# Linear attention into a SoLU layer on one core: a fourth chunk on token rows, its sums copied out of PSUM, its products on GpSimd, under a new order table

## The chip, the core and the metric

The kernel runs on one NeuronCore of a Trainium2 chip. Five engines work side by side, each through a queue of its own in strict order: TensorE (PE in the profile, its weight loads PEld), VectorE (DVE), ScalarE (ACT), GpSimd (POOL) and SyncE (SP), which here only issues DMAs. They meet through semaphores. The metric is the device time of one execution in microseconds (us). Three runs of the kernel before took 181.89, 182.10 and 182.81 us, so the median is 182.1 us.

## The reference

Inputs are q, k, v of shape 8 batches x 8 heads x 576 tokens x 64, float32, a norm weight g_norm of 64, and a layer's weights w_in (512 x 1024), w_out (1024 x 512) and g_ln (1024).

```python
kv  = einsum('bhsd,bhse->bhde', k, v)          # 64 x 64 per batch and head
o   = einsum('bhsd,bhde->bhse', q, kv)
x   = o / sqrt(mean(o*o, -1) + 1e-6) * g_norm  # per token and head
x   = x with heads side by side                # 4608 tokens x 512
h   = x @ w_in                                 # 4608 x 1024
u   = h * softmax(h)
out = (u - mean(u)) / sqrt(var(u) + 1e-6) * g_ln @ w_out
```

The whole has 4608 x 512 float32 values of output.

## The kernel before, in words

The tokens are cut into nine chunks of 512. Chunks 0 to 7 are 512 of the 576 tokens of one batch each; chunk 8 collects the 64 tokens that are left of each batch (tile `q_last`, filled by the pieces `ql0` to `ql7`, L175 or L173). Work is cut into named pieces, `o5.0` or `h6.21` for example: letters for the step, then the chunk, then the part. The steps of one chunk are

- `k`, `v`, `q`: loads, issued by POOL (L269), each 576 KB once it is bfloat16; `kv` (L314): k^T v on PE, 144 small matmuls for a whole batch; `kc`: its copies into `kvd` in SBUF;
- q turned so that features lie on partitions. Chunks 0 to 4 do it on PE (`qt`, L359, with copies `qc`). Chunks 5 to 8 do it with a DMA transpose that SP issues (`qx`, L370). All DMA transposes stand behind `gate` (L343), a one-element copy on POOL that waits for the last load, `q7`;
- `o`: q times k^T v into a two-bank PSUM tile, two halves per chunk. Two forms exist, described below; they end in x, the input of the layer;
- `h`: x times w_in on PE (L572 for chunks 0 to 2, L581 for the others), `e`: exp on ACT (L592, L599), `u`: h times exp on DVE (L607, L612), `r`: the squares' sum (L630 on ACT, L632 on DVE, for chunks 3 and up), `st` and `rs`: the row statistics, `t`: u turned by a DMA transpose that SP issues (L637, chunks 3 and up), `a`: times w_out on PE (L767), `b`: the row's scale out of PSUM (L782 ACT, L784 DVE) and `d`: the store (L799 or L801, on SP, POOL or ACT).

From `o` to x there are two forms, and a list, `ROWS_OF_X`, says which chunks have the second.

The first has features on partitions: `o` (L407, 8 matmuls of 256 columns a half), `sq` (L420, ACT), `s` (L435, PE: the heads' means by a matmul), `ln` and `ex` (L439 and L443, ACT), `x` (L453, DVE, from PSUM). It has four parts per chunk.

The second has tokens on partitions: `o` (L470, 32 matmuls of 64 columns a half), `sq` (L479, ACT, 1024 wide), `vd` (L483, DVE: sums per head), `vl` (L489 and L491, ACT), `vg` (L495, POOL: the scale times g_norm, spread to 1024 columns), `x` (L504, DVE: PSUM times that), and `xt` (L512), a DMA transpose of x that SP issues. It has two halves per chunk, and the chunk's stores go as two DMAs of half the size (L799). Chunks 6, 7 and 8 have this form.

What sets the order is one string, `ORDER`: it names every piece once, with its engine after a slash where there is a choice and its buffer after an @. `Plan.run` emits the pieces in that order, so each engine's queue is that string cut down to its pieces. Buffers are named slots: `P0` to `P2` are PSUM tiles of two banks, `S0` and `S1` of one bank, `L`, `M`, `ob` and others are SBUF slots. A piece that takes a slot waits until all users of the slot's last tile are done. The table was found by a search outside the kernel and is pasted in.

Of the kernel before, what the change touches and what calls it, by code (L numbers as in the profile page):

```python
# [8 lines left out]
FP32 = mybir.dt.float32  # L9
# [17 lines left out]
ROWS_OF_X = (6, 7, 8)  # L27
# [53 lines left out]
qc2.0/dve@M0 h1.2+@P1 h1.2 e1.0@M5 u1.0@L5 b0.2/dve@ob2 h1.3+ h1.3 e1.1@M4 u1.1 h1.4+@P0 h1.5+ k4@L3 o2.0@P2
sq2.00@osq0 sq2.01@osq1 r1.0/pool@L0 h1.4 h1.5 qt2.1@S0 e1.2@M3 s2.00@S1 qc2.1/dve ln2.00@lss0 ex2.00@rst1 h1.6+@P1
h1.7+ v4 h1.6 h1.7 e1.3@M7 u1.2 u1.3 s2.01@S1 ln2.01@lss0 a0.30@S0 o2.1@P0 sq2.10@osq1 a0.31 sq2.11@osq0 ex2.01@rst0
s2.10@S1 s2.11@P1 ln2.10@lss1 g1.0@M8 g1.1 g1.2 b0.3/dve@ob0 ln2.11@lss0 a1.00@S0 ex2.10@rst2 ex2.11@rst3 x2.00@M3
q4@M0 k5@L1 v5 x2.01 x2.10 r1.1/pool r1.2/pool r1.3/act ql3/act a1.01 kv3@P2 kc3.1/act qt3.0@S1 x2.11 h2.0@P0 h2.1
h2.2@P1 h2.3 kc3.0/act qc3.0/act@M4 d0.2/sp d0.3/sp kc3.2/act h2.4@P2 h2.5 g1.3 q5@M5 qt3.1@S1 e2.0@M9 g2.0@M7
e2.1@M10 e2.2@M11 u2.0@L4 u2.1 h2.6@P0 h2.7 e2.3@M3 g2.1 g2.2 qc3.1/dve u2.2 k6@L2 qt4.0@S1 o3.0@P1 sq3.00@osq0
qc4.0/dve@M10 r2.0/act@L6 r2.1/pool u2.3 r2.2/act z1@P2 y1 st1 rs1 b1.0/dve@ob0 d1.0/sp a1.10@S1 a1.11 a1.20@P0
r2.3/act s3.00@P2 ln3.00@lss0 a1.21 b1.1/dve@ob2 b1.2/dve@ob1 g2.3 z2@S0 sq3.01@osq0 y2 ex3.00@rst3 st2 o3.1@P2
sq3.10@osq1 s3.01@S1 ln3.01@lss0 a1.30@P0 sq3.11@osq0 ex3.01@rst2 s3.10@S0 ln3.10@lss1 ex3.10@rst0 x3.00@M4 x3.01  # L90
a1.31 a2.00@S1 s3.11@S0 ln3.11@lss0 kv4@P1 ex3.11@rst2 kc4.0/act a2.01 v6 q6@M3 k7@L0 rs2 b1.3/dve@ob3 v7 q7@M7
d1.1/sp d1.2/sp x3.10 kv5@P0 kc4.2/dve kc5.1/act kc4.1/dve o4.0@P1 sq4.00@osq0 x3.11 ql5/pool qt4.1@S0 qc4.1/act
# [32 lines left out]
def kernel(  # L125
# [16 lines left out]
    nc = tc.nc  # L142
# [14 lines left out]
    T = {}  # L157
# [700 lines left out]
```

## Time and profile before

| | |
|---|---|
| median of three runs | 182.1 us (181.89 to 182.81) |
| profiled execution: its time, its span on the core | 181.77 us, 179.7 us |
| PE, DVE, ACT, POOL busy in the span | 164.9, 127.1, 128.1, 71.9 us |
| granted PE clock | 0.999 |
| the last eight matmuls begin at, and take | 173.82 us, 1.04 us |

The profiled execution's own time is 2.07 us more than its span, which runs from the first to the last instruction. A row of the groups reads: source line, engine, operation, what it writes <- what it reads, shape and type, how many; then busy time and the mean of one in ns; then the idle time of the engine just before and what ended it. A matmul of 512 columns shows 379 ns, but matmuls overlap: in a run of them one begins every 0.216 us (16 of them take 3.45 us in the chain). PE's work is counted below at that pace and not from the busy time.

### The profile page before, as it was taken

How to read it: one execution, taken by the hardware profiler on the slowest of the kernel's cores; microseconds unless marked ns; L12 is line 12 of the kernel's file. 1: busy time of each engine (PE TensorE's matmuls, PEld its weight loads, DVE VectorE, ACT ScalarE, POOL GpSimd, SP SyncE). 2: the span in 40 equal slices, each digit the busy share in tenths (PEclk: the TensorE clock that was granted, in tenths of full speed). 3: DMA queues.
4: the chain of work that ended last, by engine and by line, in shares of the span. 5: the costliest groups of instructions: out<-in, count | busy, mean ns of one | idle time of the engine just before them, and what ended most of it. 6: DMA issues, size and time to landing. Idle time of an engine off the chain costs nothing.

```text
span 179.7 us, 4520 instructions
## 1 busy us (share of the span) xinstructions
PE 164.9 (92%) x1808; PEld 81.1 (45%) x1831; DVE 127.1 (71%) x222; ACT 128.1 (71%) x239; POOL 71.9 (40%) x83
## 2 busy tenths in 40 slices
PE   6899958699999999999998999899999999999990
PEld 3344435345435565454443444444445444444450
DVE  2327599258874776667998869999788987948630
ACT  2377794593899687979879898469979746986210
POOL 7941596040899998100140006501132960222000
PEclk9999999999999999999999999999999999999999
DMA  5999999999999999999799999999998689968994
GB/s 170 252 207 275 353 208 209 205 208 222 248 233 232 209 207 198 277 214 206 157 172 203 206 216 220 152 256 245 171 227 239 99 166 248 200 139 215 175 256 125
DMA packets 60424, 37.81 MB, mean 210 GB/s; under 512 B 42140, under 2 KB 55204, under 8 KB 60404
## 3 DMA queue, kind: packets, MB, share of 16 engines
q0 software_dynamic: 15456, 20.16, 58.1%
q1 hardware_dynamic: 44036, 15.87, 44.1%
q10 hardware_dynamic: 912, 1.51, 3.1%
q8 instruction: 14, 0.23, 0.5%
q14 instruction: 6, 0.05, 0.1%
HBM read 32.54 MB, written 9.44 MB: 234 GB/s over the span
## 4 chain that ended last, share of the span: by engine, by line
PE 63%; DMA 22%; DVE 6%; issue 3%; POOL 1%; SPq 1%; ACT 1%; POOLq 0%; DVEq 0%; ACTq 0%
PE ps_S L767 20%; PE ps_P L581 19%; DMA sb_M<-in_q_dram 9%; PE ps_P L572 8%; PE ps_P L767 5%; DMA out_dram<-sb_ob 4%; DMA sb_L<-in_v_dram 4%; DMA sb_M<-sb_M 3%; PE ps_S L359 2%; DVE sb_ob L784 2%; PE ps_P L314 2%; PE ps_P L407 2%; DMA sb_L<-sb_L 2%; PE ps_P L691 1%; PE ps_S L435 1%
## 5 line engine op out<-in xcount | busy, mean ns | idle before, releaser
L767 PE MATMUL ps_S<-w_out_sb,sb_L 128*128 128x512 bf16 x220 | 53.1, 379 | 2.9 <-issue 2.4
L581 PE MATMUL ps_P<-w_in_sb,sb_M 128*128 128x512 bf16 x188 | 42.7, 379 | 1.0 <-ACT kvd L173 0.8
L767 PEld LDWEIGHTS <-sb_L 128*128 128x128 bf16 x280 | 26.4, 98 | 33.4 <-issue 3.3
L612 DVE SCALAR_TENSOR_TENSOR sb_L<-ps_P,sb_M 128x1024 bf16<-128x1024 f32 x24 | 29.1, 1222 | 8.4 <-ACT sb_M L599 8.2
L599 ACT ACTIVATE sb_M<-ps_P 128x1024 f32<-128x1024 f32 x24 | 24.5, 1023 | 8.2 <-PE ps_P L581 7.1
L581 PEld LDWEIGHTS <-sb_M 128*128 128x128 bf16 x192 | 18.7, 98 | 23.3 <-issue 0.9
L495 POOL TENSOR_TENSOR sb_M<-rr,g_rep 128x1024 f32<-128x1024 f32 x6 | 12.3, 2061 | 30.4 <-ACT rr L491 23.7
L572 PE MATMUL ps_P<-sb_M,w_in_sb 128*128 128x512 bf16 x94 | 21.9, 379 | 0.1
L607 DVE TENSOR_TENSOR sb_L<-ps_P,sb_M 128x1024 bf16<-128x1024 f32 x12 | 14.6, 1222 | 8.2 <-ACT sb_M L592 8.2
L453 DVE SCALAR_TENSOR_TENSOR sb_M<-ps_P,g_cols,sb_rst 128x512 bf16<-128x512 f32 x24 | 18.0, 790 | 2.9 <-ACT sb_rst L443 2.6
L784 DVE TENSOR_SCALAR sb_ob<-ps_S,rstd 128x512 f32<-128x512 f32 (+1 forms) x19 | 13.8, 735 | 7.7 <-PE ps_S L767 2.2
L592 ACT ACTIVATE sb_M<-ps_P 128x1024 f32<-128x1024 f32 x12 | 12.2, 1024 | 6.9 <-PE ps_P L572 6.9
L643 POOL TENSOR_TENSOR sb_M<-sb_M 128x512 bf16<-128x512 f32 x12 | 15.1, 1278 | 4.9 <-ACT sb_M L592 4.8
L420 ACT ACTIVATE sb_osq<-ps_P 128x512 bf16<-128x512 f32 x24 | 13.4, 596 | 4.6 <-PE ps_P L407 4.6
L630 ACT ACTIVATE sb_M<-sb_L 128x1024 bf16<-128x1024 bf16 x14 | 14.6, 1047 | 0.0
L572 PEld LDWEIGHTS <-w_in_sb 128*128 128x128 bf16 x96 | 9.2, 98 | 10.5 <-issue 0.2
L801 POOL DMA_DIRECT2D out_dram<-sb_ob x10 | 6.3, 633 | 16.4 <-DVE sb_ob L784 8.8
L632 DVE SCALAR_TENSOR_TENSOR sb_M<-sb_L 128x1024 bf16<-128x1024 bf16 x10 | 12.8, 1276 | 0.1
L443 ACT ACTIVATE sb_rst<-sb_lss 128x512 f32<-128x512 f32 x20 | 12.0, 632 | 0.1
L767 PE MATMUL ps_P<-w_out_sb,sb_L 128*128 128x512 bf16 x47 | 11.4, 379 | 0.1
L206 PE MATMUL ps_S<-zeros 128*128 128x512 bf16 (+1 forms) x18 | 8.5, 591 | 1.8 <-DVE zeros L188 1.5
L624 POOL TENSOR_TENSOR sb_L<-sb_L 128x1024 bf16<-128x1024 bf16 x4 | 7.6, 1910 | 6.1 <-DVE sb_L L607 6.0
(96 smaller groups left out, 211.2 us busy)
## 6 DMA issues: line engine op xcount, KB each, us to landing
out_dram<-sb_ob SPq DMA_DIRECT2D x14, 256.0 KB, 4.2
sb_L<-in_k_dram POOLq DMA_DIRECT2D x6, 576.0 KB, 12.2
sb_L<-in_v_dram POOLq DMA_DIRECT2D x6, 576.0 KB, 13.1
sb_M<-in_q_dram POOLq DMA_DIRECT2D x6, 576.0 KB, 12.3
out_dram<-sb_ob POOLq DMA_DIRECT2D x10, 256.0 KB, 4.8
sb_L<-in_moe_w_out_dram POOLq DMA_DIRECT2D x2, 1024.0 KB, 15.8
out_dram<-sb_ob SPq DMA_DIRECT2D x10, 128.0 KB, 3.0
sb_M<-in_q_dram POOLq DMA_DIRECT2D x4, 288.0 KB, 7.0
```

Source lines behind the costliest of these rows:

```text
L420: nc.scalar.activation(out=t[:, :], in_=T["o", c, hf][:, z], func=AF.Square)
L453: nc.vector.scalar_tensor_tensor(out=T["x", c][:, pairs_of(c, hf), :, z], in0=T["o", c, hf][:, z].rearrange("p (n q) -> p n q", n=2), scal ...
L572: nc.tensor.matmul(t[:, f % 2], w_in_sb[:, dt, f * 128:(f + 1) * 128], T["x", c][:, dt].rearrange("p q z -> p (q z)"), start=(dt == 0), st ...
L581: nc.tensor.matmul(T["h", c, m][:, half], x_block(c, m, dt), w_in_sb[:, dt, half * 512:half * 512 + 512], start=(dt == 0), stop=(dt == NP ...
L599: nc.scalar.activation(out=t.rearrange("p a b -> p (a b)"), in_=T["h", c, m].rearrange("p a b -> p (a b)"), func=AF.Exp, accum_out=T["zsum ...
L607: nc.vector.tensor_tensor(out=flat(T["u", c][:, 2 * p:2 * p + 2, :]), in0=flat(T["h", c, p]), in1=flat(T["e", c, p]), op=MUL)
L612: nc.vector.scalar_tensor_tensor(out=T["un", c][:, m, :], in0=T["h", c, m].rearrange("p a b -> p (a b)"), scalar=1.0, in1=T["e", c, m].rea ...
L630: nc.scalar.activation(out=unused, in_=src, func=AF.Square, accum_out=by)
L632: nc.vector.scalar_tensor_tensor(out=unused, in0=src, scalar=1.0, in1=src, op0=MUL, op1=MUL, accum_out=by)
L643: nc.gpsimd.tensor_tensor(out=T["es", c][:, n, :], in0=e[:, 0, :], in1=e[:, 1, :], op=ADD)
L767: nc.tensor.matmul(T["acc", c, m][:, 0], T["u", c][:, f, m * 128:(m + 1) * 128], w_out_sb[:, f, :], start=(f == 0), stop=(f == NF - 1))
L784: nc.vector.tensor_scalar_mul(out=t[:, :], in0=src, scalar1=T["rstd", c][:, m:m + 1])
```

## The change

Chunk 5 joins chunks 6, 7 and 8 in the second form, with tokens on partitions. In that form a new piece `oc` copies each half's 128 x 1024 sums from PSUM to an SBUF tile in float32, on ACT or DVE as the table says (DVE for oc5.0, oc6.0, oc7.0, oc8.0 and oc8.1; ACT for oc5.1, oc6.1 and oc7.1). The product that makes x leaves DVE: GpSimd makes it from the copy, right behind `vg` in its queue. The PSUM tile is then free once `sq` and `oc` have read it. And the order table is another one from end to end: the searched table's engines, slots and order differ in nearly every place.

```diff
-ROWS_OF_X = (6, 7, 8)
+ROWS_OF_X = (5, 6, 7, 8)
...
+    def o_out(c, hf, engine):
+        T["os", c, hf] = room(("os", c, hf), [128, 1024], FP32)
+        copy(engine, T["os", c, hf][:, :], T["o", c, hf].rearrange("p x i -> p (x i)"))
+
     def x_rows(c, hf):
         if hf == 0:
             T["xr", c] = room(("xr", c), [128, 2, 1024], BF16)
-        nc.vector.tensor_tensor(
-            out=T["xr", c][:, hf], in0=T["o", c, hf].rearrange("p x i -> p (x i)"),
-            in1=T["rg", c, hf].rearrange("p i e -> p (i e)"), op=MUL,
+        nc.gpsimd.tensor_tensor(
+            out=T["xr", c][:, hf], in0=T["os", c, hf][:, :], in1=T["rg", c, hf].rearrange("p i e -> p (i e)"), op=MUL
         )
...
+            plan.add("oc" + n, ("act", "dve"), lambda e, hf=hf: o_out(c, hf, e), ["o" + n], [("M", ("os", c, hf))], [("o", c, hf)])
...
-            plan.add("x" + n, "dve", lambda hf=hf: x_rows(c, hf), ["vg" + n] + [f"x{c}.0"] * hf, [] if hf else [("M", ("xr", c))],
-                     [("o", c, hf), ("rg", c, hf)] + [("xr", c)] * hf)
+            plan.add("x" + n, "pool", lambda hf=hf: x_rows(c, hf), ["vg" + n, "oc" + n] + [f"x{c}.0"] * hf,
+                     [] if hf else [("M", ("xr", c))], [("os", c, hf), ("rg", c, hf)] + [("xr", c)] * hf)
```

Four stretches of the new table that are spoken of below. Around the second half of chunk 1:

```diff
-... o1.0@P2 warm8@S0 wc3 sq1.00@osq0 sq1.01@osq1 kv1b@P1 ... a0.00@S0 ... qt1.1@S1 kc1b.0/dve s1.00@P0 s1.01@P1 ...
+... o1.0@P2 warm8@S1 sq1.00@osq0 ... s1.00@S1 sq1.01@osq1 s1.01@P1 ... qt1.1@S0 ... kv1b@P0 ... a0.00@S1 ...
```

Around the first DMA transposes and chunk 5's `o`, cut down to SP's queue, POOL's queue and PE's queue:

```diff
-SP:   ... d0.1 d0.2 d0.3 d1.0 d1.1 d1.2 t3.0 t3.1 qx5 qx6 t3.2 ...
+SP:   ... d0.0 d0.1 d1.0 t3.0 qx5 t3.1 t3.2 d1.2 qx6 qx7 t3.3 t4.0 t4.1 t4.2 xt5.0 d2.3 xt5.1 qx8 t4.3 xt6.0 ...
-POOL: ... q7 ql5 d1.3 gate gb d2.2 ql7 vg6.0 vg6.1 d3.1 d3.2 d4.0 vg7.0 d4.1 vg7.1 vg8.0 vg8.1 d5.1 ...
+POOL: ... q7 gb d0.2 d0.3 ql1 gate d1.1 d1.3 d2.0 d2.1 vg5.0 x5.0 d2.2 vg5.1 d3.0 x5.1 ql5 vg6.0 x6.0 d3.2 vg6.1 x6.1 vg7.0 x7.0 d4.0 vg7.1 d4.2 x7.1 d4.3 vg8.0 x8.0 d5.0 vg8.1 d5.1 x8.1 d5.2 ...
-PE:   ... h4.30 h4.31 o5.0 a2.31 a3.00 ... kv6 o5.1 a3.10 ... o6.0 o6.1 ... a4.01 h5.00 h5.01 kv7 ...
+PE:   ... h3.31 s4.10 a2.20 a2.21 a2.30 s4.11 a2.31 a3.00 a3.01 o5.0 o5.1 kv7 a3.10 h4.00 ... a3.31 o6.0 o6.1 o7.0 a4.00 a4.01 a4.10 h5.00 ...
```

DVE's queue in the stretch in which GpSimd now makes x:

```diff
-DVE:  ... vd6.0 b3.2 x5.10 x5.11 vd6.1 x6.0 ql6 r4.3 kc7.0 st4 x6.1 u5.0 r5.0 ... x7.0 b5.0 vd7.1 vd8.0 b5.2 r6.1 vd8.1 x7.1 x8.0 st6 x8.1 u7.0 ...
+DVE:  ... oc6.0 vd6.0 ql2 st4 oc7.0 vd6.1 u5.0 u5.1 vd7.0 oc8.0 oc8.1 vd7.1 vd8.0 vd8.1 b4.2 u5.2 u5.3 r5.2 u6.0 ... u6.3 st5 b5.0 b5.1 u7.0 u7.1 r6.0 r6.2 st6 r7.0 u7.2 ...
```

And the end, where the last chunk's two half-width stores change queues:

```diff
-... b8.3|0/dve@ob1 d8.2/act b8.3|1/dve@ob2 d8.3|0/act d8.3|1/sp
+... b8.3|0/dve@ob4 a8.3|1@S1 b8.3|1/dve@ob3 d8.2/act d8.3|0/sp d8.3|1/sp
```

PE has 88 instructions more than before, POOL 17 more, DVE 4 fewer, ACT 1 fewer, and SP as many.

104 lines of the change are left out of this document (52 added, 52 removed).

## The prediction

> **What bounds the kernel now.** I read the page's busy lines and slices first, then the chain that ended last, then the groups by form, and then the queues of DVE, POOL and SP where the change touches them.
>
> ```profile
> PE 164.9 (92%) x1808; PEld 81.1 (45%) x1831; DVE 127.1 (71%) x222; ACT 128.1 (71%) x239; POOL 71.9 (40%) x83
> ...
> PE   6899958699999999999998999899999999999990
> ...
> DVE  2327599258874776667998869999788987948630
> ACT  2377794593899687979879898469979746986210
> POOL 7941596040899998100140006501132960222000
> ...
> DMA packets 60424, 37.81 MB, mean 210 GB/s; under 512 B 42140, under 2 KB 55204, under 8 KB 60404
> ```
>
> PE is at nine tenths in nearly all slices; DVE and ACT fill many slices of the second half to eight or nine; POOL is nearly idle from about the twentieth slice on. The chain tells PE's own pace and the places where it stood:
>
> ```profile
> 31.68 0.32 PE ps_S L767
> 32.00 1.73 issue
> 33.73 0.59 PE ps_S L767 x2
> ...
> 45.97 0.34 PE ps_P L407 x8
> ...
> 49.67 0.21 PE ps_S L435
> ...
> 54.80 0.70 PE ps_P L314 x72
> ...
> 61.23 0.45 PE ps_S L359 x8
> ...
> 64.19 1.23 PE ps_P L691 x80
> ...
> 92.04 5.72 DMA sb_M<-sb_M
> ...
> 97.81 0.41 PE ps_P L407 x8
> ...
> 115.31 0.37 ACT kvd L173
> ...
> 115.72 8.79 PE ps_P L581 x40
> ...
> 125.31 0.45 PE ps_P L470 x32
> ...
> 131.04 3.45 PE ps_S L767 x16
> ```
>
> A 512-column matmul starts every 3.45/16 = 0.216 us. Counting PE's whole queue at the paces of such rows gives 152.9 us of work: 137.6 from the first `a0.00` (it begins at 31.6) to the last matmul's end (174.9), so waits in that stretch are 143.3 - 137.6 = 5.7 us. Of these 1.73 are the stop at 32.0, where nothing in the kernel is waited for; about 0.4 stand before 97.81 (`o5.0`, for the DMA transpose `qx5`) and 0.75 before 115.72 (`h5.10`, behind late copies of `kv7`). A kernel that waits so little can win 5.7 us at the very most there and can lose without limit. What counts is which waits the new table removes and which it makes.
>
> **Chunk 5's form.**
>
> ```profile
> L420 ACT ACTIVATE sb_osq<-ps_P 128x512 bf16<-128x512 f32 x24 | 13.4, 596 | 4.6 <-PE ps_P L407 4.6
> L439 ACT ACTIVATE sb_lss<-ps_S 128x512 f32<-128x512 f32 x13 | 7.7, 598 | 0.8 <-PE ps_S L435 0.7
> L443 ACT ACTIVATE sb_rst<-sb_lss 128x512 f32<-128x512 f32 x20 | 12.0, 632 | 0.1
> L453 DVE SCALAR_TENSOR_TENSOR sb_M<-ps_P,g_cols,sb_rst 128x512 bf16<-128x512 f32 x24 | 18.0, 790 | 2.9 <-ACT sb_rst L443 2.6 <-ACT sb_rst L447 0.2
> L479 ACT ACTIVATE sb_rst<-ps_P 128x1024 bf16<-128x1024 f32 x6 | 6.0, 1016 | 1.1 <-PE ps_P L470 1.1
> L483 DVE TENSOR_REDUCE ms<-sb_rst 128x16 f32<-128x1024 bf16 x6 | 7.2, 1212 | 1.2 <-ACT sb_rst L479 1.2
> L504 DVE TENSOR_TENSOR sb_M<-ps_P,sb_M 128x1024 bf16<-128x1024 f32 x6 | 7.2, 1215 | 0.0
> L592 ACT ACTIVATE sb_M<-ps_P 128x1024 f32<-128x1024 f32 x12 | 12.2, 1024 | 6.9 <-PE ps_P L572 6.9
> L607 DVE TENSOR_TENSOR sb_L<-ps_P,sb_M 128x1024 bf16<-128x1024 f32 x12 | 14.6, 1222 | 8.2 <-ACT sb_M L592 8.2
> L489 ACT ACTIVATE lv<-ms 128x16 f32<-128x16 f32 x6 | 1.3, 213 | 0.2 <-DVE ms L483 0.2
> L643 POOL TENSOR_TENSOR sb_M<-sb_M 128x512 bf16<-128x512 f32 x12 | 15.1, 1278 | 4.9 <-ACT sb_M L592 4.8
> L624 POOL TENSOR_TENSOR sb_L<-sb_L 128x1024 bf16<-128x1024 bf16 x4 | 7.6, 1910 | 6.1 <-DVE sb_L L607 6.0
> ```
>
> On PE, 2 x 0.34 for `o` and 4 x 0.215 for the head means go, and 2 x 0.45 come: 0.68 + 0.86 - 0.90, or 0.64 us less. PE is the bound, so this counts in full: **-0.6**.
>
> ACT loses 4 x (596 + 598 + 632) = 7.3 us and gets 2 x (1016 + 2 x 213) = 2.9 and three copies. No copy of 128 x 1024 float32 out of PSUM is in the trace; ACT's exp of that shape takes 1.02 us, so 3.1: ACT ends 1.3 lighter. DVE loses 4 x 790 + 6 x 1215 = 10.4 us and gets 2 x 1212 and five copies at most at the 1222 of a product of that size: 8.5, so 1.9 lighter. Both reliefs lie beside PE and I price them at nothing by themselves; PE's work covers them, and without that cover they would be worth at most their 1.3 and 1.9.
>
> POOL gets two more `vg` and eight products. Each product reads two SBUF tiles of 1024: 1.9 us by the bfloat16 row, at most 2 x 1278 by the float32 row of half that width. I take 1.9, as width and operand count are the same there: about 19 us more on POOL, nearly all after 97. POOL has that much idle time, but the two are now one after the other, so x is ready 1.9 - 1.2 = 0.7 us later after `vg`, and a store on POOL's queue that waits for its `b` holds the next product up. In the new queue `x7.0` has `d4.0`, `x8.0` has `d5.0` ahead of what follows; all have their `b` in time as I walk the queue.
>
> The transpose `xt5` adds two entries to SP's queue and chunk 5's stores become eight halves instead of four. They stand beside PE with several us to spare, except `xt5.0`, which waits behind `t4.2`; I count it at nothing (its end of the range is +1 us, if `h5.00` has to wait for it).
>
> **The head.** In the new table `s1.00`, `s1.01` and `qt1.1` come before `kv1b`. That is 2 x 0.215 + 0.45 = 0.88 us of work. The stop of 1.73 us at 32.0 stands after some 700 instructions of PE; PE's queue holds the same up to `o1.0`, so the 700th now lies inside `kv1b`. If the stop ends at the same time, 33.7, PE has by then done 0.88 more, and lacks the rest of `kv1b` and one matmul: **-0.4**. The ends are nothing and -1.7 (the stop is gone).
>
> **Chunk 5's `o` and the first transposes.** `o5.0` waited for `qx5`, which stands behind `gate`, which waits for the last load.
>
> ```profile
> 88.83 0.18 POOL L343 COPY sb_L<-sb_M 1x1 bf16<-1x1 bf16 x1 [13.32 <-DMA sb_M<-in_q_dram]
> ```
> ```profile
> 89.04 2.84 SPq L637 DMA_TRANSPOSE sb_L<-sb_L  x2
> 92.04 4.10 SPq L370 DMA_TRANSPOSE sb_M<-sb_M  x1
> ```
>
> `qx5` was issued at 92.04 and landed at 97.77, 5.7 us later. The new order issues it behind one transpose instead of two (1.4 us sooner), and four stores (256 KB each) that were issued before the last load now come after it; at the page's mean of 210 GB/s a store is 1.2 us, so the gate opens 0 to 5 us sooner. I take half, 2.5: `qx5` lands at 97.77 - 1.4 - 2.5 = 93.9, and 0.4 later as it now shares the DMA engines with those stores. But the new table also puts `o5.0` earlier: PE has 73.6 us of work ahead of it instead of 77.2, and with the 0.4 from the head it is ready near 97.4 - 3.6 - 0.4 = 93.4. So the wait is about 0.9 instead of 0.4: **+0.5**, from -0.4 (the gate opens early) to +2.6 (it doesn't).
>
> **PSUM tiles.** With the copy a half's tile is free after `sq` and `oc` instead of after `x`; 2 to 3 us of holding go. But `sq` now decides, and ACT's queue is full there: `o7.1` takes the slot of `o7.0`, whose square is the last of six ACT instructions of 1024 columns (with `sq6.0`, `oc6.1`, `sq6.1`, `e5.0`, `e5.1`), with `vl6.0`, `rs4` and `b4.0` between: 6 x 1.02 + 0.8 + 0.6 = 7.5 us, and ACT comes to them about 1.2 us late, behind three squares' sums of chunk 4. PE has ten pieces of 4 x 0.216 = 0.86 us there, 8.6. With a few tenths for ACT's own waits: **+0.3** (0 to 0.9). In chunk 3, `s3.10` now waits for `ln3.01`. ACT has between the end of `h2.7` and that point 1 exp, 2 copies (0.37 each), 2 squares of 1024 (as L479), 4 `sq`, 2 `ln` and 1 `ex`: 1.0 + 0.7 + 2.0 + 2.3 + 1.2 + 0.6 = 7.8 us; PE has `kv3`, `a1.10` to `a1.21`, both `o3`, two head means, `z2` and `a1.30`: 0.7 + 3.5 + 0.7 + 0.4 + 1.2 + 0.9 = 7.4 us. **+0.4**. Against these, the 0.75 before 115.72 came from DVE's queue ahead of `kv7`'s copies, which is rearranged: **-0.75**.
>
> **POOL and DVE at once.** This is the step on which I put most weight, because the trace shows that the two engines block each other.
>
> ```profile
> L632 DVE SCALAR_TENSOR_TENSOR sb_M<-sb_L x10: 1212/1222/1781, 86.5 to 165.9; 128x1024 bf16<-128x1024 bf16 x10
> ```
> ```profile
> L495 POOL TENSOR_TENSOR sb_M<-rr,g_rep x6: 1892/1901/2878, 107.9 to 142.8; 128x1024 f32<-128x1024 f32 x6
> ```
> ```profile
> 111.91 1.51 DVE L175 COPY q_last<-sb_M 128x256 bf16<-128x256 bf16 x1
> ```
>
> The squares' sum on DVE takes 1.22 us, and 1.78 in the one case that began while POOL made a `vg`; the `vg` behind it took 2.88 instead of 1.90; and a copy from SBUF to SBUF that takes 0.22 elsewhere took 1.51 beside another `vg`, just ahead of the copies of `kv7`. Products out of PSUM (L504, L607) don't show this. The Trainium skill (SBUF — State Buffer, Who interferes with whom) gives the rule: a DVE instruction with two SBUF inputs, or in a two-port mode, and a GpSimd instruction that reads SBUF lock each other out for a whole instruction. The trace agrees, by 0.56, 0.98 and 1.29 us.
>
> From `vg5.0` to `x8.1` POOL now has 16 such instructions, 30 us of a stretch of some 45. In DVE's queue `ql2`, `st4`, `r5.2`, `st5`, `r6.0`, `r6.2` and `st6` fall into it: seven meetings, with a chance of 30/45 and half an instruction, 0.95 us, each: 4.4 us of delay on DVE, and each `r` that comes first holds POOL up by as much as 1.2. DVE is at eight to nine tenths there, so a part of it reaches PE through `u` and the P slots: `u6.0` behind `r5.2` is the place that I find, for `h6.30` takes the slot that `u6.0` frees. I take **+1.0**, a quarter, as the seven meetings have slack of 1 to 3 us but for that one; the ends are 0 and 4.4.
>
> **The tail.**
>
> ```profile
> 174.02 0.48 DVE L784 TENSOR_SCALAR sb_ob<-ps_S,rstd 128x256 f32<-128x256 f32 x1 [1.85 <-PE ps_S L774]
> ```
> ```profile
> 174.32 2.46 ACTq L799 DMA_DIRECT2D out_dram<-sb_ob  x4
> ```
>
> Both last half-width stores go on SP: four issues of 2.46/4 = 0.61 one after the other from 174.50, so the last begins at 176.3 where ACT's last began near 176.1: **+0.2** (0 to 0.5).
>
> **The sum** against the profiled execution, 181.77: -0.64 - 0.4 + 0.5 + 0.3 + 0.4 - 0.75 + 1.0 + 0.2 = +0.6, or 182.4. That run stands 0.33 under the median of 182.1, so on the median's scale I forecast **182.7 us**.
>
> **Rivals.** First, *the table carries it* (faster): none of the added waits comes, since the gate opens 5 us sooner and the meetings of DVE and POOL fall into slack. Then -0.64 - 0.4 - 0.4 - 0.75 + 0.2 is -2.0, and 180.1 us; with part of the waits some 180.8. For it speaks that DVE and ACT are lighter and that PSUM is freed sooner; against it that only 5.7 us of waits exist. Second, *the lock decides* (slower): DVE's delay of 4.4 us reaches PE whole, 182.7 + 3.4 = 186.1; with half of it, 2.2, 183.9. It decides once DVE's slack between two `u` is below one POOL instruction, 1.9 us. POOL's low share in the slices speaks against it, DVE's digits for it. The Trainium skill (GPSIMD Engine Reference, Performance versus the Vector engine) speaks against the move as well: it has about 2.5 cycles an element for two inputs, which for 1024 elements at its 1.2 GHz is an estimate of 2.1 us a product and 1.8 us more on POOL in all; no run so far shows this product. Third, *the gate doesn't move*: the wait for `qx5` is 2.1 us longer than I take it, 184.8. Against it: four stores really do move behind the last load.
>
> **How the numbers follow.** Chances: the forecast's case (181.7 to 183.8) 0.40, the table carries it 0.32, the lock decides 0.15, the gate doesn't move 0.13. A measurement here tells 0.5% from no change, that is 181.2 to 183.0. Of the first case 0.24 lie within that and 0.16 above; of the second 0.30 are below it and 0.02 within; the others are above. So faster 0.30, same 0.26, slower 0.44. The range from 180.2 to 185.6 leaves out the far ends of the rivals, about 2 in 10.
>
> **What the profile after would show.** The sum is right if PE's waits after its first `a` are 6 to 7 us; if L470 shows 256 matmuls and L435 20; if DVE's L632 and its SBUF copies show several instructions far above 1.22 and 0.22 us beside POOL's; if `gate` runs at 86 to 87; and if the stop near 33 is under 1 us. It is wrong if the product on POOL takes clearly more than 1.9 us without DVE beside it, if the last load lands at 88.7 as before, or if a long stop at "issue" stands in another place of PE's queue.

## The result, and the profile after

The changed kernel takes **190.87 us** (median of 4 runs, 189.18 to 192.88) against 182.45 for the kernel before on the same chip (181.89 to 183.34): a ratio of 1.0426, with a 95% interval of 1.0337 to 1.0514. Forecast were 182.7 us, with a range up to 185.6. The loss is some 8 us.

The profiled execution is the slowest of the four (192.88 us, span 191.1), and the four differ in TensorE's granted clock: its mean was 0.999 in the run of 189.18 and 0.968 in this one. So a part of the 11.4 us between the two profiled spans, and of the waits below, belongs to that one execution.

The page of the changed kernel, with the same rows as before and the one of the granted clock:

```profile
PE 169.0 (88%) x1852; PEld 82.6 (43%) x1875; DVE 128.5 (67%) x217; ACT 128.5 (67%) x238; POOL 98.5 (52%) x103
...
PE   6789978999999998999499995999759999989990
...
PEclk9999999999999999999969998899988999999998
DMA  5999999999999999997999999946498499999994
...
L508 POOL TENSOR_TENSOR sb_M<-sb_M,sb_M 128x1024 bf16<-128x1024 f32 x8 | 18.9, 2357 | 2.8 <-ACT sb_M L634 2.5
...
L636 DVE SCALAR_TENSOR_TENSOR sb_M<-sb_L 128x1024 bf16<-128x1024 bf16 x10 | 17.0, 1728 | 0.1
```

VectorE and ScalarE are hardly changed. GpSimd is 26.6 us busier, of which the eight products are 18.9. What is new on TensorE are the holes in its row, at slices 20, 25, 29 and 30, and a clock below 9 behind each. Where in the span that is, and how much, is read from stretches of 12 us. The columns are the stretch, its length, each engine's busy time (and instructions), the granted clock, the DMA share and the rate. Before:

```profile
core 0: us, PE busy (x) PEld busy (x) DVE busy (x) ACT busy (x) POOL busy (x), PEclk, DMA share, GB/s
86.00:98.00 12.00, 11.58 (x60) 5.14 (x59) 11.44 (x22) 10.07 (x19) 2.81 (x4) 1.00 0.89 173
98.00:110.00 12.00, 11.68 (x195) 5.78 (x191) 9.52 (x17) 11.19 (x24) 1.90 (x1) 1.00 1.06 216
110.00:122.00 12.00, 11.20 (x121) 5.20 (x120) 11.36 (x19) 7.29 (x18) 3.13 (x3) 1.00 1.13 198
...
sum 72.00, PE 69.99 PEld 33.07 DVE 62.61 ACT 57.05 POOL 20.55; mean PE 11.66 PEld 5.51 DVE 10.44 ACT 9.51 POOL 3.43
```

The same of the changed kernel (both run on to 158):

```profile
86.00:98.00 12.00, 9.03 (x170) 4.57 (x170) 8.26 (x16) 6.71 (x13) 2.84 (x5) 0.96 0.91 211
98.00:110.00 12.00, 11.95 (x49) 5.19 (x50) 9.85 (x19) 10.93 (x24) 7.97 (x6) 0.90 1.19 200
110.00:122.00 12.00, 9.93 (x128) 4.39 (x129) 7.83 (x15) 7.25 (x14) 6.90 (x5) 0.86 1.10 199
...
134.00:146.00 12.00, 8.81 (x33) 3.52 (x32) 9.77 (x13) 5.64 (x14) 7.58 (x6) 0.86 0.89 204
...
sum 72.00, PE 63.19 PEld 28.75 DVE 55.35 ACT 49.93 POOL 42.74; mean PE 10.53 PEld 4.79 DVE 9.23 ACT 8.32 POOL 7.12
```

In the 72 us from 86 on TensorE idles 8.8 us where it idled 2.0, and the clock's deficits (0.04 + 0.10 + 0.14 + 0.14) x 12 make another 5.0. Together that is 11.8 us more, about the whole difference of the spans. In the 86 us ahead of them TensorE is busy 78.28 us against 78.11, so the loss does not lie there. What TensorE waited for from 85 to 158, in the view of its waits:

```profile
PE ps_P L585 <- DVE sb_L L616: 3.3, 3, 2.2
PE ps_P L470 <- DMA sb_M<-sb_M: 2.8, 1, 2.8
PE ps_P L585 <- DMA sb_M<-sb_M: 2.0, 1, 2.0
```

These are three long stops: `o5.0` for the transposed load of q5 (2.8), `h5.00` for the transposed x of chunk 5 (2.0), and `h6.30` for `u6.0` on VectorE (2.2 of the 3.3). Behind each TensorE runs at half clock: after the third, 8 matmuls of 512 columns take 3.56 us, 0.44 each instead of 0.216. A clock of 0.86 over 12 us is 3.4 us at half (0.14 x 12 / 0.5), and costs 1.7. The chain through the first two, followed back from 120 us:

```profile
78.89 7.50 DMA out_dram<-sb_ob
...
88.06 7.66 DMA sb_M<-sb_M
...
95.76 0.71 PE ps_P L470 x64
...
110.75 5.88 DMA sb_M<-sb_M
...
116.67 3.65 PE ps_P L585 x10
```

Of 38 us of this chain 21 are three transfers: a store of 7.5 us, which holds an output buffer that ScalarE needs, q5's transpose (7.7) and the first of chunk 5's x (5.9). The DMA row of the page is at 9 in all of these slices but one (the nineteenth). It was so before the change too (at 9 in every slice from 90 to 134 us):

```profile
DMA  5999999999999999999799999999998689968994
```

The third stop is the one at which VectorE and GpSimd block each other; VectorE's timeline, then GpSimd's:

```profile
136.61 3.63 DVE L636 SCALAR_TENSOR_TENSOR sb_M<-sb_L 128x1024 bf16<-128x1024 bf16 x1
...
140.18 1.21 DVE L616 SCALAR_TENSOR_TENSOR sb_L<-ps_P,sb_M 128x1024 bf16<-128x1024 f32 x1
```

```profile
136.79 2.36 POOL L508 TENSOR_TENSOR sb_M<-sb_M,sb_M 128x1024 bf16<-128x1024 f32 x1
```

`r5.2`, 1.22 us alone, takes 3.63: the product's 2.36 lies whole inside it, and `u6.0` waits behind.

### The profile page after: what moved, and what is told of

Its sections match the earlier page's. It is cut to its first block, busy times and chain, and to the rows that moved or that the text cites. A ratio compares the mean times of both kernels' runs of the same rounds, so it can differ in the third digit from the quotient of the medians.

```text
span 191.1 us, 4622 instructions
## 1 busy us (share of the span) xinstructions
PE 169.0 (88%) x1852; PEld 82.6 (43%) x1875; DVE 128.5 (67%) x217; ACT 128.5 (67%) x238; POOL 98.5 (52%) x103
## 4 chain that ended last, share of the span: by engine, by line
PE 40%; DMA 26%; issue 10%; DVE 10%; ACT 7%; POOL 3%; SPq 1%; DVEq 0%; POOLq 0%
PE ps_S L771 13%; PE ps_P L585 12%; DMA sb_M<-sb_M 9%; DMA sb_M<-in_q_dram 8%; PE ps_P L576 6%; DMA sb_L<-in_v_dram 4%; DMA out_dram<-sb_ob 4%; DVE sb_L L616 3%; DVE sb_M L636 2%; PE ps_P L771 2%; DVE ms L483 2%; ACT sb_M L603 2%; SPq L641 1%; POOL sb_M L647 1%; DVE a L718 1%
## 5 line engine op out<-in xcount | busy, mean ns | idle before, releaser
L771 PE MATMUL ps_S<-w_out_sb,sb_L 128*128 128x512 bf16 x229 | 56.5, 383 | 1.0 <-issue 0.4
L585 PE MATMUL ps_P<-w_in_sb,sb_M 128*128 128x512 bf16 x188 | 47.8, 405 | 6.4 <-DVE sb_L L616 3.3
L771 PEld LDWEIGHTS <-sb_L 128*128 128x128 bf16 x280 | 26.6, 98 | 31.8 <-issue 1.9
L495 POOL TENSOR_TENSOR sb_M<-rr,g_rep 128x1024 f32<-128x1024 f32 x8 | 15.2, 1903 | 24.4 <-ACT rr L491 16.8
L508 POOL TENSOR_TENSOR sb_M<-sb_M,sb_M 128x1024 bf16<-128x1024 f32 x8 | 18.9, 2357 | 2.8 <-ACT sb_M L634 2.5
L453 DVE SCALAR_TENSOR_TENSOR sb_M<-ps_P,g_cols,sb_rst 128x512 bf16<-128x512 f32 x20 | 15.2, 789 | 3.0 <-ACT sb_rst L443 2.6
L636 DVE SCALAR_TENSOR_TENSOR sb_M<-sb_L 128x1024 bf16<-128x1024 bf16 x10 | 17.0, 1728 | 0.1
L420 ACT ACTIVATE sb_osq<-ps_P 128x512 bf16<-128x512 f32 x20 | 11.0, 596 | 2.8 <-PE ps_P L407 2.8
L175 DVE COPY sb_M<-ps_P 128x1024 f32<-128x1024 f32 (+1 forms) x7 | 7.4, 1067 | 7.1 <-PE ps_P L470 3.4
L479 ACT ACTIVATE sb_rst<-ps_P 128x1024 bf16<-128x1024 f32 x8 | 8.0, 1028 | 5.0 <-DVE sb_M L175 5.0
L786 ACT ACTIVATE sb_ob<-ps_S,rstd 128x512 f32<-128x512 f32 x15 | 9.9, 682 | 1.6 <-PE ps_S L771 1.3
```

Of the source, the lines that this page charges most:

```text
L453: nc.vector.scalar_tensor_tensor(out=T["x", c][:, pairs_of(c, hf), :, z], in0=T["o", c, hf][:, z].rearrange("p (n q) -> p n q", n=2), scal ...
L495: nc.gpsimd.tensor_tensor(out=t[:, :, :], in0=T["rr", c, hf][:, :, None].to_broadcast([128, 16, D]), in1=g_rep[:, None, :].to_broadcast([1 ...
L508: nc.gpsimd.tensor_tensor(out=T["xr", c][:, hf], in0=T["os", c, hf][:, :], in1=T["rg", c, hf].rearrange("p i e -> p (i e)"), op=MUL)
L585: nc.tensor.matmul(T["h", c, m][:, half], x_block(c, m, dt), w_in_sb[:, dt, half * 512:half * 512 + 512], start=(dt == 0), stop=(dt == NP ...
L636: nc.vector.scalar_tensor_tensor(out=unused, in0=src, scalar=1.0, in1=src, op0=MUL, op1=MUL, accum_out=by)
L771: nc.tensor.matmul(T["acc", c, m][:, 0], T["u", c][:, f, m * 128:(m + 1) * 128], w_out_sb[:, f, :], start=(f == 0), stop=(f == NF - 1))
```

## The experiments

Each ran beside the kernel before, whose median in the five groups was 182.2 to 182.6.

### One suspect at a time

The first theory was that the product on GpSimd makes the loss, by way of VectorE's blocked instructions. The rivals were the slow clock, the stores ahead of q5's load, and the new table itself.

**one_input**

```
-  nc.vector.scalar_tensor_tensor(out=unused, in0=src, scalar=1.0, in1=src, ..., accum_out=by)
+  nc.vector.tensor_reduce(out=by, in_=src, op=ADD, axis=mybir.AxisListType.X)
```

> The changed kernel, but every squares' sum on DVE (ten of them) is a plain sum of the same tile with one SBUF input instead of the product of two; so the sum of squares and with it the variance is left out for those rows, and the row statistics' first term has its sign turned. The plain sum of that width took 1.21 us on DVE in all eight cases of the changed kernel, beside GpSimd or not. Theory A (GpSimd's products lock DVE out): the 3.6 us instruction becomes 1.2, the pause of PE of 2.6 us before h6.30 goes and with it the half clock behind it, in all 3 to 5 us: 186 to 188. Theory B (the late DMA transposes of chunk 5 cost the time, the lock only uses up slack): the pauses before o5.0 and h5.00 stay and the time is 189.5 to 191.5. Under both, the pauses before o5.0 (2.8) and h5.00 (2.0) stay.

Measured: 190.47 us, ratio 1.045 (1.040 to 1.050). All ten of these sums took 1.21 to 1.22 us, so the blocking of `r5.2` was gone, and the time was not. TensorE's waits from 85 to 158:

```profile
PE ps_P L585 <- DMA sb_M<-sb_M: 3.8, 2, 2.7
PE ps_P L470 <- DMA sb_M<-sb_M: 2.4, 1, 2.4
PE ps_S L771 <- DVE vare L724: 1.8, 1, 1.8
```

The stop moved on by one piece of TensorE's queue: h of chunk 7 now waits 2.7 us for its transposed x, and the clock goes to half behind that one. The blocking decides the place of a stop, and hardly the end.

**filled**

```
+  plan.add(f"fill{i}", "pe", lambda i=i: fill(i), ...)   # 12, 10 and 10 matmuls of zeros
-  o5.0@P2 ... h5.00@P2 ... h6.30@P0
+  fill0@P2 o5.0@P2 ... fill1@P2 h5.00@P2 ... fill2@S0 h6.30@P0
```

> The changed kernel, with 12, 10 and 10 matmuls of zeros (0.216 us each, 6.9 in all) put into PE's queue where it paused: before o5.0, before h5.00 and before h6.30. Nothing is left out. Theory C (a pause of PE of over 2 us is followed by 3.4 us at half clock, which costs 1.7 us each): the clock stays at 1.0 through, the waits themselves stay, and the time is near that run of the changed kernel that had a mean clock of 0.999, 189.2: 188.5 to 189.7 instead of a median of 190.9. The rival (the half clock comes from elsewhere, such as the load on the chip): the three stretches at 0.5 stay and the time is 190.5 to 192.

Measured: 190.32 us, ratio 1.044 (1.039 to 1.049), mean clock 0.999: the half-clock stretches were gone, and the ratio is no lower than the 1.043 of the changed kernel. So the slow clock follows the pauses, and with it gone the loss stays. How much it costs by itself this run cannot tell, since the fills take time too: `o5.0` began at 96.55 behind its fill and at 95.76 without it, `h5.00` at 117.59 and at 116.67.

**stores_later**

```
-  d1.1/pool ... d1.3/pool d2.0/pool ... d2.1/pool ... x5.1 xt5.1 ql5/pool
+  ... x5.1 xt5.1 d1.1/pool d1.3/pool d2.0/pool d2.1/pool ql5/pool     (4 output buffers more)
```

> The changed kernel, but the four stores d1.1, d1.3, d2.0 and d2.1, which GpSimd issues just behind the gate, stand behind x5.1 in its queue (with four more store buffers, so that nothing waits for them). Theory B1 (these stores share the DMA engines with qx5 and hold it up: it took 7.7 us to land instead of 5.7): qx5 lands 1.5 to 2 us sooner, PE's pause before o5.0 falls from 2.8 to about 1 us, no half clock follows, and the time falls by 3 to 3.7: 187 to 188. Rival (qx5 is slow because of SP's own queue and the transposes ahead of it): it lands at 95.7 as before and the time stays at 189.5 to 191.5.

Measured: 189.17 us, ratio 1.035 (1.028 to 1.043). The pause before `o5.0` fell from 2.8 to 0.1 us, but the one before `h5.00` grew from 2.0 to 3.1, with the half clock behind it. That was the first sign of what the loss is: with the four stores elsewhere in the same full stretch, another transfer was late.

**old_table_gpsimd**

```
   # the kernel before and its table; chunks 6 to 8:
+  plan.add("oc" + n, ("act", "dve"), lambda e, hf=hf: o_out(c, hf, e), ["o" + n], [("M", ("os", c, hf))], ...)
-  plan.add("x" + n, "dve", ...)
+  plan.add("x" + n, "pool", ...)
```

> The kernel before with its own table and three chunks on token rows, and one part of the change alone: the sums of chunks 6, 7 and 8 are copied out of PSUM behind sq (oc6.0, oc7.0, oc8.0 and oc8.1 on DVE, oc6.1 and oc7.1 on ACT) and GpSimd makes the product from the copy behind vg. Theory A (the product on GpSimd costs the time wherever it stands): slower than before by 2 to 5 us, 184.5 to 187.5, with L632's instructions on DVE over 2 us beside it. Rival (the new table and chunk 5's transposes cost the time): 182 to 183.5, as DVE is lighter by six products of 1.2 and heavier by four copies of 1.2.

Measured: 190.43 us, ratio 1.049 (1.042 to 1.056). Put like this into a table that was not made for it, the new form of three chunks costs as much as the whole change. The next group takes it apart.

### The form's parts, in both tables

**old_table_copies**

```
   # old_table_gpsimd, but
-  nc.gpsimd.tensor_tensor(out=T["xr", c][:, hf], in0=T["os", c, hf][:, :], ...)
+  nc.vector.tensor_tensor(out=T["xr", c][:, hf], in0=T["os", c, hf][:, :], ...)
```

> The kernel before, its table kept, with the six copies of the sums of chunks 6 to 8 to SBUF added (three on ScalarE, three on VectorE, about 1.1 us each) and the product still on VectorE, which reads the copy in place of PSUM. If GpSimd's product made the 8 us of the kernel that had the same copies and the product on GpSimd, this one is 182 to 184.5: the copies are 3.3 us of work on each of two engines that are busy two thirds of the time. If copying is what delays the chain of chunks 6 to 8, it is above 187.

Measured: 189.08 us, ratio 1.037 (1.029 to 1.045). The six copies of 1.0 to 1.2 us, together with products that read them from SBUF, already cost 6.6 us in the old table; the run does not part the two. Its timeline of TensorE shows one stop of 3.25 us at 140.7, behind an eviction on VectorE (line 788), which stands behind copies and sums of squares in that queue. One product on VectorE, which now reads SBUF alone, took 2.92 us beside GpSimd's scale; the six out of PSUM had 1.215 on the mean.

**old_table_one_input**

```
   # old_table_gpsimd with the sum of one_input
```

> The old table with copies and products on GpSimd (190.4 us), the sum of squares on VectorE replaced by a sum with one input (the sum of squares is left out, the sign of its use turned). If VectorE's waits beside the product (L636 2.94 and 2.81, L718 1.97, L724 1.82 us, against 1.2 and 0.1 to 0.2 alone) are the cost, it comes to 184.5 to 187. If the cost is the longer chain on GpSimd itself (scale 1.9 us, product 2.36 us, then a transpose of 5.2 us, ahead of h of the same chunk), it stays at 188.5 to 191.

Measured: 188.44 us, ratio 1.035 (1.031 to 1.039), 2.0 us under the kernel that it is made from: by the medians VectorE's blocked sums are a quarter of the loss in that table.

**product_on_vector**

```
   # the changed kernel, but
-  plan.add("x" + n, "pool", ...)      nc.gpsimd.tensor_tensor(...)
+  plan.add("x" + n, "dve", ...)       nc.vector.tensor_tensor(...)
```

> The changed kernel with one thing undone: the products of chunks 5 to 8 are made on VectorE again (line 508), from the same copy in SBUF, at the same places of the same table. If the product's place on GpSimd is the cause, whether by the time it takes there (2.36 us), by GpSimd's queue behind it or by VectorE waiting beside it, most of the 8 us comes back: 182.5 to 185.0. If the cause is the rest of the change (the new table, chunk 5's transposed load, the copies), it stays at 187 to 191; VectorE then has 8 products more, about 1.2 us each, on a queue that is busy 128 of 189 us.

Measured: 201.26 us, ratio 1.105 (1.099 to 1.112), a miss for both theories. In this table the product on GpSimd is 10 us better than on VectorE, where it stands at its place in the queue and holds up the sums and evictions behind it (2.1 us of VectorE's idle time are products waiting for the scale, and the trace has GpSimd's next scales wait 33.5 us and ScalarE's exps 13.3 us for these products; that this makes the 10 us is my reading, and no run shows it). So "the product went to the slower engine" is no account of the loss.

**latency**

```
   # the changed kernel with one_input's sum and stores_later's order, and
-  t4.1 t4.2 vg5.0@M2 x5.0@M12 xt5.0@M0
+  vg5.0@M2 x5.0@M12 xt5.0@M13 t4.1 t4.2
```

> The changed kernel with three of its waits taken away together: the sum of squares with one input (no long VectorE wait before h6.30), the stores of chunks 1 and 2 off the SP and GpSimd queues ahead of the load of q5 (d1.1, d1.3, d2.0, d2.1 behind x5.1), and xt5.0 ahead of t4.1 and t4.2 on SP. If the waits add up, each counted once, 2.8 before o5.0, 2.0 before h5.00 and 3.2 before h6.30 with the slow clock behind them (1.7 each): 182 to 185. If a wait that is taken away is replaced by the next product's (h7.00 waiting for xt7.0, as the run with one input had it), 186.5 to 189.

Measured: 188.19 us, ratio 1.032 (1.024 to 1.040). Three waits were taken away and, by the medians, 2.7 us came back. At 110.7 TensorE now stopped 2.2 us for the transposes of u in chunk 4 that `xt5.0` had passed, and at 138.1 it stopped 2.5 us for VectorE's u.

### Leaving the chain out

**no_copies**

```
-  ... oc5.0/dve@M1 ... oc8.1/dve@M8
-  in0=T["os", c, hf][:, :], in1=T["rg", c, hf]...
+  in0=T["rg", c, hf]..., in1=T["rg", c, hf]...
```

> The changed kernel without the eight copies out of PSUM (five on VectorE at 1.22 us, three on ScalarE at 1.0): GpSimd multiplies the scale with itself, so that its instructions keep their number, shape and place. The sums' content is left out. If the work of the copies on the two filled engines is what makes the time (six of them in the old table gave +6.6 us without any product on GpSimd), it comes to 183 to 186. If the length of the chain on GpSimd (1.9 + 2.36 us) and the transposes behind it make it, it stays at 188.5 to 191.

Measured: 188.78 us, ratio 1.035 (1.029 to 1.041). By the medians the copies are worth some 2 us in the new table, but the intervals of the two ratios overlap.

**no_product**

```
-  vg5.0@M2 x5.0@M12 ...  vg8.1@M10 ... x8.1
-  nc.sync.dma_start_transpose(T["x", c][:, hf], T["xr", c][:, hf])
+  nc.sync.dma_start_transpose(T["x", c][:, hf], T["os", c, hf][:, :])
```

> The changed kernel with the scale and the product left out for chunks 5 to 8: the copy out of PSUM writes the bf16 rows itself, and the transpose reads them. The norm of q k^T v and its gains are left out; copies, sums of squares, transposes, stores and the table stay. If GpSimd's part of the chain (4.3 us for each half of a chunk, its queue, and VectorE's waits beside it) is what makes the time, nearly all of it goes: 181 to 184.5. If the copies, the order of the stores and loads, or the transposes themselves make it, it stays at 186 to 190.

Measured: 194.82 us, ratio 1.067. Slower with work left out was an artefact: a copy's slot was now held until the transpose had read it, and an instruction of chunk 6 on ScalarE waited 7.4 us for that slot. It is mended in **no_product_slots**:

```
-  oc7.0/dve@M6 ...
+  oc7.0/dve@M17 ...     (each copy a slot of its own)
```

> The kernel that leaves out scale and product of chunks 5 to 8 (the copy writes the bf16 rows, the transpose reads them), mended in one thing: the copies have slots of their own, six more. In the run before, e6.0 had to wait for the slot of the copy of chunk 7 until its transpose had read it (ScalarE waited 7.4 us, TensorE 5.46). With that artefact gone: 181.5 to 184.5 if GpSimd's 4.3 us in each half chunk is what makes the loss; 186 to 189 if the waits that do not go through GpSimd (qx5's load at 92.6, xt5.0 behind t4.2 on SP, the copies on VectorE) make it.

Measured: 188.17 us, ratio 1.027 (1.019 to 1.034). With nothing left of GpSimd's part of the chain, two thirds of the loss are still there. TensorE's waits are 3.9 us for q5's load, 4.1 for transposes of x, and 0.9 for VectorE: nearly DMA alone.

**no_product_5** leaves out scale and product for chunk 5 only.

> The same for chunk 5 alone, the chunk that the change newly puts on token rows; chunks 6 to 8 keep scale and product on GpSimd. If chunk 5's chain is what is late (h5.00 waits 2.0 us for xt5.0, with the slow clock behind it worth 1.7), that stop goes and GpSimd has 8.6 us less ahead of chunk 6: 185.5 to 187.5. If chunks 6 and 7 carry the loss by themselves, 189 to 191.

Measured: 190.49 us, ratio 1.044 (1.036 to 1.051): no difference.

**no_xt5** leaves out chunk 5's two transposes as well:

```
-  copy(engine, T["os", c, hf][:, :], ...)   ... xt5.0@M0 ... xt5.1
+  copy(engine, T["x", c][:, hf], ...)       # h5 reads what the copy wrote
```

> The changed kernel with the rest of chunk 5's new chain gone: its scale and product are left out as in the run for chunk 5 alone (190.5 us), and now its two transposes too: the copy out of PSUM writes what h5 reads. The transposes are 2 x 1024 packets of 26 ns over 16 engines, 3.3 us of full DMA engines. If these and the wait of h5.00 for xt5.0 are the price of putting chunk 5 on token rows: 184 to 187. If 188.5 or more, what is left of the loss lies in chunks 6 to 8 and in q5's load.

Measured: 189.42 us, ratio 1.044 (1.037 to 1.051). The stop before `h5.00` was gone and the time nearly the same: the stops for q5's load (3.9) and for `u6.0` (2.2) stayed.

**relieved** is no_product_slots with the stores later, and with `xt5.0`, `xt5.1` and `xt7.0` further ahead on SP.

> The same, and also the queues cleared: the stores d1.1, d1.3, d2.0 and d2.1 behind chunk 5's transposes, those transposes (xt5.0, xt5.1) right behind qx7 on SP, and xt7.0 ahead of t5.1. Copies, sums of squares and the order of TensorE stay. If the loss is the sum of GpSimd's chain and SP's queue, it is 180 to 183, as before or below. If it stays above 185, neither makes it, and the order of TensorE's work with the copies on VectorE and ScalarE is left.

Its four runs lay between 186.4 and 193.5 us, too far apart for a verdict. In the profiled one (186.42) TensorE waited 5.2 us for the transposes of u that had now been passed, and no more for those of q and x.

**mended** computes everything: stores_later, and

```
-  r5.2/dve ... r6.0/dve ... r6.2/dve
+  r5.2/act ... r6.0/act ... r6.2/act
```

> The changed kernel computing all that it should, with the four stores moved behind x5.1 and three of VectorE's sums of squares that were caught beside the product (r5.2, r6.0, r6.2; 3.63, 1.61 and 3.50 us against 1.22) given to ScalarE (1.05 us). If each wait that goes is followed by the next, as in the runs so far (gains of 1.7 and 0.5 for these two alone): 187.5 to 189.5. If the waits beside the product were the last thing in chunks 6 and 7: 184 to 187.

Measured: 189.91 us, ratio 1.038 (1.030 to 1.047), no better than stores_later alone. VectorE's wait before `h6.30` was gone, and TensorE waited 5.4 us for transposes of x instead.

**before_ql6_pool** tried for a version better than both: in the kernel before, `ql6/dve` became `ql6/pool`.

> The kernel before with one copy of 128x256, ql6, on GpSimd in place of VectorE, where it took 1.51 us beside GpSimd's scale at 111.9 and made kv7 wait 0.75 us. If that wait ends with it: 181.3 to 182.0, a gain of 0.4 to 0.8. If the scale of chunk 6 behind it on GpSimd is late by the copy's own time (0.40) and the wait moves to h6: 182.2 to 182.8.

Measured: 182.11 against 182.32 us, ratio 0.9996 (0.9964 to 1.0028): no difference.

### The bytes

In most runs in the new table the longest wait that was left, or that came next, was one for a DMA transpose. The view of DMA from 86 to 122 us shows what they share the engines with. Before:

```profile
q1 hardware_dynamic: 19708, 5.61, 87.8%
q0 software_dynamic: 615, 1.37, 14.1%
...
out_dram<-sb_ob SPq DMA_DIRECT2D x4, 256.0 KB, 3.4
out_dram<-sb_ob POOLq DMA_DIRECT2D x3, 256.0 KB, 4.8
sb_L<-sb_L SPq DMA_TRANSPOSE x9, 3.4
sb_M<-sb_M SPq DMA_TRANSPOSE x5, 5.4
```

The changed kernel:

```profile
q1 hardware_dynamic: 19948, 5.44, 90.2%
q0 software_dynamic: 543, 1.79, 15.6%
...
out_dram<-sb_ob POOLq DMA_DIRECT2D x7, 256.0 KB, 4.2
out_dram<-sb_ob SPq DMA_DIRECT2D x3, 256.0 KB, 3.9
sb_L<-sb_L SPq DMA_TRANSPOSE x8, 4.2
sb_M<-sb_M SPq DMA_TRANSPOSE x6, 5.4
```

The shares of the two queues add up to 102% and 106%: the 16 engines are full in both. The numbers of transposes are the same (15, with the one of `q_last`), and those of q and x take 5.4 us from issue to landing in both; the stores are ten instead of seven. The last pair of runs changes nothing but bytes.

**few_stores**

```
+  if c in (0, 1, 2, 3, 4):
+      queue.dma_start(rows_of(c, m)[0:4][:, :, cols], T[key][0:8, :])
+  elif c in ROWS_OF_X: ...
```

> The changed kernel with the stores of chunks 0 to 4 cut to a sixteenth (8 of 128 partitions of each tile; the other rows of the output are left unwritten). No instruction, queue or wait moves; only some 5 MB less goes through the 16 DMA engines, of which a part lies in the stretch from 86 to 122 where their busy share is 1.0 to 1.2. If it is the full DMA engines that make q5's transposed load take 7.7 us, and those of chunks 4 and 5 5 to 6 us: 184 to 187. If it is the order on the queues and the engines: 189 to 191.

**before_few_stores** is the same cut in the kernel before.

> The same cut in the kernel before, as its control: its DMA engines are as full (1.0 to 1.15 from 90 to 132), but TensorE waits for a transpose only once there, 0.4 us at 97. If TensorE is its bound: 181 to 182.5. If a full DMA costs it too, without showing as a wait: below 180.

Measured: the changed kernel falls to **184.15 us**, ratio 1.014 (1.008 to 1.020); the kernel before stays at 181.96 against 182.28 (0.998 to 1.004). By the ratios, each against its own group, the loss falls from 4.3% to 1.4%, which is 5 of 8 us; by the two medians it is 6.7. No other run gave back as much, and this one moved no instruction. The view of DMA from 86 to 122 us and that of TensorE's waits from 85 to 160, of few_stores:

```profile
q1 hardware_dynamic: 20933, 5.28, 90.1%
q0 software_dynamic: 221, 0.12, 2.1%
...
sb_L<-sb_L SPq DMA_TRANSPOSE x8, 3.8
sb_M<-sb_M SPq DMA_TRANSPOSE x7, 3.2
```

```profile
PE ps_P L585 <- DVE sb_L L616: 3.2, 3, 2.1
PE ps_P L585 <- ACT sb_rst L479: 0.6, 1, 0.6
```

By the medians the transposes of q and x land 3.2 us after their issue instead of 5.4, and TensorE waits for no transfer any more. SP's own issue of q5's transpose, in the changed kernel and then in few_stores:

```profile
88.06 5.76 SPq L370 DMA_TRANSPOSE sb_M<-sb_M  x1
```

```profile
86.45 2.73 SPq L370 DMA_TRANSPOSE sb_M<-sb_M  x1
```

It takes half as long, and begins 1.6 us sooner, as the last load landed sooner too: `gate` began at 83.78 instead of 85.75. So of the 2.8 us before `o5.0`, 1.6 went with the earlier issue and the rest with the faster transfer. The stretches of the span of few_stores:

```profile
86.00:98.00 12.00, 11.24 (x181) 5.68 (x182) 10.60 (x22) 9.34 (x17) 0.61 (x2) 1.00 0.90 160
98.00:110.00 12.00, 11.90 (x146) 5.80 (x146) 9.69 (x14) 11.84 (x26) 9.91 (x7) 1.00 1.03 166
110.00:122.00 12.00, 11.95 (x145) 6.06 (x145) 9.31 (x16) 10.40 (x20) 9.20 (x6) 1.00 0.86 129
122.00:134.00 12.00, 8.93 (x41) 3.91 (x40) 11.90 (x14) 7.52 (x16) 9.94 (x7) 1.00 0.69 121
134.00:146.00 12.00, 11.63 (x45) 4.73 (x45) 9.13 (x15) 7.08 (x18) 6.15 (x5) 0.86 0.47 91
```

From 86 to 122 TensorE idles 0.9 us, less than the 1.5 before the change, with the full clock. What is left are two waits for VectorE, 3.1 us idle from 122 to 134, and 1.7 of slow clock behind the longer one (2.1), where `r5.2` takes 3.51 us beside the product. With the slow clock that is 4.8 us, enough for the 4.1 by which the span of this profiled execution (185.56 us) is longer than that of the kernel before; the medians differ by 1.9.

So the loss has two parts. The larger, some 5 to 7 of 8 us, goes with the bytes of the stores, by way of late transposes and a late last load; the rest fits the stop behind `r5.2`, though no run takes both away. The kernel before has the same full DMA engines and the same 5.4 us for a transpose and loses nothing by them; as I read it, because it asks for no transposed result so soon (its one wait for a transfer there is the 0.4 before `o5.0`). The run cannot tell whether it is the engines' time or something else on the stores' way that the stores take from the transposes: in few_stores the two queues still add up to 92%. Nor was it tried to reorder the whole table for more lead.

## Why the prediction was wrong, point by point

- **TensorE's work, -0.6:** right in the counts. L470 shows 256 matmuls and L435 15 + 5.
- **The head, -0.4:** the stop near 33 is gone but for waits under 0.4 us, as forecast. TensorE was ready for `o5.0` at 93.0 instead of 97.4, 4.4 sooner, of which the text's count of work explains 3.6: the term was there, and 0.8 rather than 0.4.
- **The gate:** right to a tenth. It was to open 2.5 us sooner, with `qx5` issued at 88.1; it was issued at 88.06. That it fits so well is luck in part, since 2.5 was the middle of a range from 0 to 5. The rival "the gate doesn't move" falls. So does "the table carries it", which wanted 5 us and no added wait.
- **`o5.0`'s wait, +0.5:** the first step that failed. TensorE was ready at 93.0 (forecast 93.4), but the transfer was taken 0.4 longer than before for sharing the DMA engines with four stores, and took 1.9 longer (7.66 against 5.72). It landed at 95.7 instead of 94.3, and the wait was 2.8 instead of 0.4: +2.4 in place of +0.5, near the end of +2.6 that the text gave for another reason, a gate that doesn't move.
- **`xt5.0`, counted at nothing with an end of 1 us:** the second step that failed. It stands behind `t4.2` as the text said, took 5.88 us from its issue at 110.75, and `h5.00` waited 2.0.
- **The slow clock** is no term of the sum at all. No trace of before had it between 85 and 179; the view of its stretches shows the full clock. In this execution it took 5.0 us, in the fastest of the four (mean clock 0.999) next to nothing.
- **PSUM and ScalarE, +0.3 and +0.4; the wait of 0.75 for kv7, gone:** the last is gone; the other two don't show among TensorE's waits.
- **The lock, +1.0:** the mechanism and the place were right to the instruction (`u6.0` behind `r5.2`, then `h6.30`): 2.2 us and the slow clock behind it. The size was not, as the product is 2.36 us and not 1.9, and a sum that meets it waits for more than half of it. By the Trainium skill (SBUF — State Buffer, Who interferes with whom) the two lock each other out for a whole instruction: the trace agrees (3.63 = 1.22 + 2.36 but for 0.05), and even an instruction of 128x4 elements (line 718) took 2.35. The rival "the lock decides" (186.1) nevertheless was not what happened: with the lock's place cleared the time stayed at 190.5.
- **The product, 1.9:** 2.34 to 2.37 in all eight. The float32 row of half the width, 2 x 1278, was nearer than the bfloat16 row that was taken. So was the estimate of 2.1 from the Trainium skill (GPSIMD Engine Reference, Instruction dispatch), which has approximately 2.5 cycles an element for two inputs; the section that the prediction names, Performance versus the Vector engine, measured 2.6.
- **The tail, +0.2:** it didn't come. Between the last matmul and the end lie 4.6 us, and 4.8 before.

Against the sum, `o5.0` has 1.9 us more than forecast, `h5.00` 2.0, the lock 1.2 and the slow clock 5.0. That is 10.1 of the 10.5 us by which the profiled execution (192.88) lies above the sum (182.4); the smaller terms that didn't come stand against some of it.

What failed as a whole is that transfers were priced by the mean rate of the page (210 GB/s, "1.2 us a store") and not by how full the DMA engines already are. The page of before has them at 9 in every slice from 90 to 134; the prediction quoted the slices of four engines and not that row. In such a stretch the stores made the transposes late (5.4 us against 3.2 with few stores), and a kernel that newly waits for these transposes pays on TensorE.

## What to carry to other kernels

Read the DMA row beside the engines' rows: where it is at 9, a transfer that is added or moved can make others late, and a result that TensorE needs soon after a transpose has to be priced with the latency in that stretch, not with the transfer's own. When no single wait gives the time back, cut the bytes of a transfer nobody waits for, in both kernels: it moves nothing else, and the control tells whether the unchanged kernel was bound by it too. A full DMA row alone is no loss: the kernel before had it as well, and gained nothing from fewer bytes. Taking out one wait at a time shows little where the next one stands a microsecond behind.

## What was unexpected on the chip

- A pause of TensorE of 2.0 to 2.8 us was followed by 3.4 us at half clock in all three places of the profiled execution. Other pauses were not: 2.2 and 2.5 us in the run named latency, and 3.25 in old_table_copies, which had the full clock from 6 to 186 us. The same stop of 3.25 us in old_table_gpsimd was followed by the half clock (16 matmuls in 6.36 us instead of 3.61), so the length of a pause alone does not decide. The Trainium skill (TensorE: Matmul & The Clock Gate, What's actually happening) has a window of about 3.4 us that runs freely and lowers the clock after an idle one. The length agrees; the pauses that sufficed are shorter than a window, and in one run a pause of nearly its length did not suffice.
- A product on VectorE with both inputs in SBUF was held up beside GpSimd (2.92 us against 1.22), while those with one input in PSUM were not (L504, 1.215 on the mean). Copying the sums out of PSUM so exposes a product on VectorE to a wait that it did not have.
- In this table the same eight products cost 10 us more on VectorE (201.3) than on GpSimd (190.9), though most of them take half as long there (median 1.22 us against 2.36).
